# Stacked 128-row products in a delta-rule recurrence: two products over 64 rows each become one over 128

## The chip, the cores and the metric

The kernel runs on one core of one Trainium2 chip. The metric is the device time of a run in microseconds (us). The kernel before has a median of 845.26 us over three runs (835.6 to 846.0).

Engines are named as the profile names them: PE is the matrix engine (its weight loads have a row of their own, PEld), DVE the vector engine, ACT the scalar engine, POOL the general engine, SP the engine that issues most DMAs. PSUM is the memory that PE writes to; it is read by DVE and ACT.

## The reference, cut to what matters

Two blocks follow one another. The first is a recurrence over 768 time steps for 4 batches x 8 heads, with a 40 x 40 state per head:

```python
for t in range(S):
    y[:, :, t] = einsum('bhd,bhde->bhe', r_t, state)
    Sa = einsum('bhde,bhe->bhd', state, a_t)
    state = state * w_t[:, :, None, :] - einsum('bhd,bhe->bhde', Sa, b_t) + einsum('bhd,bhe->bhde', v_t, k_t)
```

The second takes the rows of y (3072 tokens of 320 numbers), routes each to the one of 8 experts whose gate logit is largest, and gives `gate_w * (relu(x @ w1[e]) @ w2[e])`. All of it is in fp32.

## The kernel before, in words

**Chunks and units.** The 768 steps are cut into 12 chunks (c) of 64 steps (T2). A unit is a chunk of two batches, so there are two units (s = 0, 1) in each chunk, 24 in all. A unit has 16 heads: 8 groups g times 2 parities par. Parity 0 lies on partitions 0 to 63 and parity 1 on partitions 64 to 127; `own(par)` is a parity's half and `oth(par)` the other half. Almost every matrix product is one head's: at most 64 rows (the contraction), 64 output partitions and 32 to 104 columns. `mm` (L228) records them all, so they share one line in the profile and are told apart by their output: ps_ntb, ps_gtk and so on. One product of fp32 shows as two MATMULs and two LDWEIGHTS. By the partitions of its input and of its output a product of 64 rows and 64 columns sits in one of four quadrants of the PE array.

**What a unit computes.** `decay` scans the decays (PT, on DVE), scales a by them into ai (POOL) and scales k and b by the reciprocals (DVE L287, POOL L290). Then:
- the system. `ntb` multiplies b with ai and an identity (16 products, 104 columns); its triangular part goes to pair (DVE L361), its other parts to off and nb (ACT L372, L374). `level` 0 to 4 (16 products each) squares and accumulates to invert the triangular system: PE into ps_lv, ACT copies to pair (L391), DVE transposes into N (L341) and adds (L394). `couple` and `whole` finish the inverse F. Systems need nothing of the state.
- the rest. `gtk` multiplies k with ai, giving GT and nk; `atv` multiplies v with r, giving AT and nv. `right` forms the right side q from the state and from GT, nv; `solve` and `zgram` give uT, u and ZT; `state` adds the products nk*nv and nb*u to the state (two products per head into one accumulation); `yield_y` adds three products per head (s*r, nk*AT, nb*ZT); its end copies y on ACT (L541) and scales it by PT on POOL (L542). `turned` transposes the state. `emit` turns y into token rows with the gate logits beside them, 16 products per unit, and sends them to x_rows with SP.

**The order of the work.** PE, DVE and ACT follow an order that is written out by hand. `weave` takes the system pieces of chunk c + 1 (16 pieces of 16 products: eight stages, two units each) and puts the products of chunk c's rest between them: after each two system products two of the rest, and what is left of the share of 26 after the piece. Tasks of `decay` for chunk c + 2 are put one after each piece from the third on. Eleven such woven steps follow one another; the last chunk's rest has no systems beside it. PE runs strictly in this order.

**PSUM.** Systems use the tag "two": two buffers of two banks, so that the two units take turns. The rest uses the tag "one": four buffers of one bank.

**After the recurrence** (L703 on) routing is computed, and from about 545 us on the experts run: layer1 (L859, L868), layer2 (L884).

Of the kernel before, what the change touches and what calls it, by code (L numbers as in the profile page):

```python
# [8 lines left out]
F32 = mybir.dt.float32  # L9
# [12 lines left out]
def kernel(  # L22
# [102 lines left out]
    with tc.tile_pool(name="ring", bufs=1) as ring, \  # L125
# [4 lines left out]

        G = 2 * NP
# [15 lines left out]
        kb_r = tiles("kb", 2, [128, 2, 2, NP, T2])  # L147
# [5 lines left out]
        nk_r = tiles("nk", 2, [128, G, 64])  # L153
# [38 lines left out]
        def preset_rest():  # L192
# [5 lines left out]
            for t in [r[0] for r in nk_r + q_r + st_r + s_r] + [r[1] for r in nk_r]:  # L198
                nc.gpsimd.memset(t[:, :, D:], 0.0)
# [5 lines left out]
        iw = ring.tile([128, NP, D + E], F32, name="iw")  # L205

        def preset_last():
            for par in range(2):
                nc.gpsimd.tensor_copy(iw[own(par), :, :D], i40[own(par), None, :].to_broadcast([64, NP, D]))
                nc.sync.dma_start(  # L210
                    iw[own(par, D), :, D:], moe_w_gate.rearrange("(p a e) x -> a e p x", p=NP, a=2)[par],
                )

        def wide(name):

            t = pp.tile([128, 2, 512], F32, name=name, tag="two", bufs=2)
            return t[:].rearrange("q b (g x) -> q (b g) x", x=128)

        def bank(name, w, gs=G):
            return pp.tile([128, gs, w], F32, name=name, tag="one", bufs=4)  # L220

        def halves(name):

            ps = [bank(name, T2 + D, NP) for _ in range(2)]
            return ps, lambda h, g: ps[g // NP][h, g % NP, :]
# [13 lines left out]
        def load(u):  # L239
# [7 lines left out]
            for b2 in range(2):  # L247
                src = packed[2 * s + b2, c * T2 // C, :, :, :, :, c * T2 % C : c * T2 % C + T2]
                for par in range(2):
                    for i, n in enumerate((K, B_)):  # L250
                        q.dma_start(d["kb"][own(par, D), b2, i], src[par, :, n])
                    q.dma_start(d["a"][own(par, D), b2], src[par, :, A])

        def load_vr(u):
# [4 lines left out]
            for b2 in range(2):  # L259
                src = packed[2 * s + b2, c * T2 // C, :, :, :, :, c * T2 % C : c * T2 % C + T2]  # L260
                for par in range(2):
                    gs = slice(b2 * NP, b2 * NP + NP)
                    nc.sync.dma_start(d["v"][own(par, D), gs], src[par, :, V])
                    nc.sync.dma_start(d["ri"][own(par, D), gs, :T2], src[par, :, R])

        def decay(u):
# [7 lines left out]
            def scan():  # L274
                PT = d["PT"] = sb.tile([128, G, T2 + 1], F32, name=f"PT{s}", bufs=3)
                d["wi"] = sb.tile([128, 2, NP, T2], F32, name="wi", bufs=2)
# [8 lines left out]
            def inverse(h, p):  # L285
                wi = d["wi"]
                nc.vector.reciprocal(wi[:, h, p : p + 2], by_batch(d["PT"][:, :, 1:])[:, h, p : p + 2])  # L287
                if p:
                    for i in (1, 0):
                        nc.gpsimd.tensor_tensor(d["kb"][:, h, i], d["kb"][:, h, i], wi[:, h], op=ALU.mult)  # L290
            return [scan] + [lambda h=h, p=p: inverse(h, p) for h in range(2) for p in range(0, NP, 2)]

        def kb(d, i, g):
            return d["kb"][:, g // NP, i, g % NP, :]


        def gtk(u):
# [3 lines left out]
            ps, at = halves("ps_gtk")  # L301
            ts = [lambda g=g, par=par: mm(at(oth(par), g), kb(d, 0, g)[own(par, D)], d["ai"][own(par, D), g, :])
                  for g, par in HD]

            def end():
                nk = d["nk"] = nk_r[s][c % 2]
                t = d["GT"] = sb.tile([128, G, T2], F32, name=f"GT{s}")
                for h in range(2):
                    gs = slice(h * NP, h * NP + NP)
                    nc.scalar.copy(t[:, gs], ps[h][:, :, :T2])  # L310
                    nc.scalar.copy(nk[:, gs, :D], ps[h][:, :, T2:])
                nc.gpsimd.tensor_tensor(t[:], t[:], up64[:, None, :].to_broadcast([128, G, T2]), op=ALU.mult)
            return ts, end

        def atv(u):
# [3 lines left out]
            ps, at = halves("ps_atv")  # L319
            ts = [lambda g=g, par=par: mm(at(oth(par), g), d["v"][own(par, D), g, :], d["ri"][own(par, D), g, :])  # L320
                  for g, par in HD]

            def end():
                nv = d["nv"] = sb.tile([128, G, D], F32, name=f"nv{s}")
                t = d["AT"] = sb.tile([128, G, T2], F32, name=f"AT{s}")
                for h in range(2):
                    gs = slice(h * NP, h * NP + NP)
                    nc.scalar.copy(nv[:, gs], ps[h][:, :, T2:])
                    nc.scalar.copy(t[:, gs], ps[h][:, :, :T2])
                nc.gpsimd.tensor_tensor(t[:], t[:], up64[:, None, :].to_broadcast([128, G, T2]), op=ALU.mult)  # L330
# [19 lines left out]
        def ntb(u):  # L350

            c, s = u
            d = units[u]
            ps = wide("ps_ntb")
            ts = [lambda g=g, par=par: mm(ps[oth(par), g, : T2 + D], kb(d, 1, g)[own(par, D)], d["ai"][own(par, D), g, :])
                  for g, par in HD]

            def end():
                old = new_pair(d, s)
                nt = d["nt0"] = old[:, :2]  # L360
                nc.vector.tensor_tensor(  # L361
                    parts(nt), ps[:, :, :T2].rearrange("q g (a t) -> q g a t", a=2),
                    nup[:].rearrange("q (a t) -> q a t", a=2)[:, None].to_broadcast([128, G, 2, 32]), op=ALU.mult,
                )
                new_n(d, s, nt)
                new = new_pair(d, s)
                nc.gpsimd.tensor_tensor(new[:, 2], old[:, 0], old[:, 1], op=ALU.add)
                nc.gpsimd.tensor_tensor(new[:, 2], new[:, 2], i32[:, None, :].to_broadcast([128, G, 32]), op=ALU.add)
                off = d["off"] = off_r[s][0]
                for par in range(2):  # L370
                    qs = own(par, 32)
                    nc.scalar.activation(off[qs, :, 32:], ps[qs, :, 32:T2], AF.Copy, scale=-1.0)  # L372
                t = d["nb"] = sb.tile([128, G, D], F32, name=f"nb{s}", bufs=2)
                nc.scalar.copy(t[:], ps[:, :, T2 : T2 + D])  # L374
            return ts, end

        def level(u, k):
# [7 lines left out]
                ps[oth(par), g, at].rearrange("q (a t) -> q a t", t=32), N[oth(par), g].rearrange("q a t -> q (a t)"), rhs[oth(par), :, g, :])  # L385
# [19 lines left out]
        def couple(u):  # L405
# [4 lines left out]
            ts = [lambda g=g, par=par: mm(ps[oth(par), g, :32], d["off"][oth(par), g, :], d["D"][oth(par), 0, g, :])  # L410
# [9 lines left out]
        def whole(u):  # L420
# [4 lines left out]
                ps[oth(par), g, :T2].rearrange("q (a t) -> q a t", a=2), d["x"][oth(par), g, :], d["TT"][oth(par), :, g, :])  # L425
# [10 lines left out]
        def right(us):  # L436

            pss = [bank("ps_q", D) for u in us]
            for u, ps in zip(us, pss):
                c, s = u  # L440
                d = units[u]
                if c:
                    yield [lambda g=g, par=par: mm(
                        ps[oth(par), g, :], d["ai"][own(par, D), g, :T2], st_r[s][0][own(par, D), g, :D],
                        start=(g == 0), stop=False, free=True) for g, par in HD], lambda ps=ps: parted(ps)
            for u, ps in zip(us, pss):
# [3 lines left out]
                def end():  # L450
# [3 lines left out]
                    ps[oth(par), g, :], d["GT"][oth(par), g, :], d["nv"][oth(par), g, :],  # L454
                    start=(c == 0), free=True) for g, par in HD], end

        def solve(u):

            c, s = u
            d = units[u]  # L460
            ps = bank("ps_uT", T2)
            ts = [lambda g=g, par=par: mm(ps[own(par), g, :], d["q"][oth(par), g, :], d["F"][oth(par), g, :])
                  for g, par in HD]

            def end():
                t = d["uT"] = sb.tile([128, G, T2], F32, name="uT", bufs=2)
# [527 lines left out]
```

## Time and profile before

| | before |
|---|---|
| median of 3 runs | 845.26 us (835.6 to 846.0) |
| the profiled execution, its own time | 844.75 us |
| its span in the profile | 843.0 us |
| mean granted PE clock | 0.954 |
| PE busy | 709.9 us, 84% of the span, 16816 MATMULs |
| DVE, ACT, POOL busy | 332.9, 282.6, 364.4 us |
| first system products of the woven steps | 66.9, 104.8, 145.4, 191.7, 236.5, 277.5, 319.5, 359.3, 402.4, 443.4, 485.5 us |
| last product of the last system | 524.2 us |

The profile page gives, for one execution, each engine's busy time and its share of the span; the span in 40 slices (busy tenths, and the granted PE clock in tenths of full speed); the DMA queues; the chain of work that ended last; and groups of instructions with count, busy time and mean duration, followed by the idle time before them and what ended it. "issue" stands for time in which an engine waited for nothing that the profile shows. Matmuls overlap, so the busy time of a group is less than its count times its mean. The windows view gives, for a stretch of time, its length, then the busy time and number of instructions of PE, PEld, DVE, ACT and POOL, the granted PE clock, the DMA share and GB/s.

### The profile page before, as it was taken

To read this page: it belongs to the slowest core of one execution; us is meant where nothing else is said; L and a number is where in the kernel's file an instruction comes from. 1 tells how busy PE (TensorE), PEld (TensorE's weight loads), DVE (VectorE), ACT (ScalarE), POOL (GpSimd) and SP (SyncE) were. 2 spreads that over 40 slices of the span, in tenths; PEclk is the share of its full clock that TensorE was granted. 3 is DMA by queue.
4 is the path that set the end of the run, shared out by engine and by line. 5 is a ranking of instruction groups with operands and counts; after the bars stand their busy time and mean duration, and the time that the engine had idled before them with its cause. 6 is when DMAs were issued, how large, how long until landed. Compare 5 with 4: busy or idle time off the path is not lost.

```text
span 843.0 us, 37380 instructions
## 1 busy us (share of the span) xinstructions
PE 709.9 (84%) x16816; PEld 576.3 (68%) x16816; DVE 332.9 (39%) x582; ACT 282.6 (34%) x752; POOL 364.4 (43%) x442
## 2 busy tenths in 40 slices
PE   0478898889897979888889898609999999999995
PEld 0478788889787979787879788604654655655653
DVE  2384565643746465656555642252110110120110
ACT  0236453534463636353636364300111111111110
POOL 9676655553656564655554633243203202111001
PEclk9998999976999999999998999858999999999998
DMA  4213132322222323232320110293325235232000
GB/s 105 51 43 76 44 87 55 86 50 52 59 63 63 74 45 76 51 70 51 70 51 23 35 23 5 54 318 93 105 81 176 90 95 170 79 96 90 16 7 24
DMA packets 123381, 61.20 MB, mean 73 GB/s; under 512 B 103697, under 2 KB 119059, under 8 KB 123220
## 3 DMA queue, kind: packets, MB, share of 16 engines
q1 hardware_dynamic: 112868, 48.34, 22.3%
q0 software_dynamic: 3136, 9.46, 3.6%
q8 instruction: 133, 2.18, 1.1%
q10 hardware_dynamic: 7216, 1.00, 0.7%
q14 instruction: 28, 0.23, 0.1%
HBM read 50.09 MB, written 9.32 MB: 70 GB/s over the span
## 4 chain that ended last, share of the span: by engine, by line
PE 48%; issue 35%; POOL 7%; DVE 4%; DMA 4%; ACT 1%; SPq 1%; POOLq 0%; ACTq 0%; DVEq 0%
PE ps_lv L228 11%; PE ps_y L228 6%; PE ps_ntb L228 5%; PE ps_q L228 4%; PE ps_atv L228 4%; PE ps_gtk L228 3%; POOL out_dram L889 3%; PE ps_f L228 3%; PE ps_z L228 3%; PE ps_x L228 3%; PE ps_S L228 2%; PE ps_uT L228 2%; PE ps_s L228 2%; POOL xg L836 1%; DMA w<-in_moe_w_dram 1%
## 5 line engine op out<-in xcount | busy, mean ns | idle before, releaser
L228 PE MATMUL ps_lv<-pair,N 64*64 64x96 f32 (+2 forms) x3840 | 201.6, 244 | 28.5 <-issue 19.4
L228 PEld LDWEIGHTS ps_lv<-pair,N 64*64 64x64 f32 x3840 | 171.1, 137 | 34.0 <-issue 24.5
L884 PE MATMUL zp<-w,h_sb 128*128 128x320 f32 (+1 forms) x512 | 124.1, 433 | 0.0
L889 POOL DMA_INDIRECT out_dram<-zo,s_idx x28 | 27.9, 998 | 210.3 <-ACT zo L888 209.7
L341 DVE STREAM_TRANSPOSE N<-pair 128x512 f32<-128x512 f32 x120 | 84.2, 701 | 66.2 <-ACT pair L391 64.9
L884 PEld LDWEIGHTS zp<-w,h_sb 128*128 128x128 f32 (+1 forms) x512 | 80.5, 177 | 37.1 <-issue 2.4
L874 DVE TENSOR_SCALAR h_sb<-hp 128x448 f32<-128x448 f32 x32 | 20.0, 625 | 209.3 <-PE hp L868 132.3
L868 PE MATMUL hp<-xgT,w 128*128 128x448 f32 x256 | 101.4, 549 | 0.0
L290 POOL TENSOR_TENSOR kb<-kb,wi 128x256 f32<-128x256 f32 x96 | 68.9, 739 | 56.2 <-DVE wi L287 52.2
L287 DVE RECIPROCAL wi<-PT 128x128 f32<-128x128 f32 x96 | 88.0, 921 | 0.1
L228 PE MATMUL ps_ntb<-ai,kb 40*64 40x104 f32 x768 | 62.4, 288 | 28.9 <-POOL ai L281 26.9
L868 PEld LDWEIGHTS hp<-xgT,w 128*128 128x128 f32 x256 | 47.8, 192 | 53.1 <-issue 53.1
L391 ACT COPY pair<-ps_lv 128x512 f32<-128x512 f32 x96 | 56.7, 590 | 77.4 <-PE ps_lv L228 65.0
L228 PEld LDWEIGHTS ps_ntb<-ai,kb 40*64 40x64 f32 x768 | 47.0, 154 | 29.5 <-POOL ai L281 26.9
L875 ACT ACTIVATE h_sb<-hp 128x448 f32<-128x448 f32 x32 | 17.4, 544 | 142.8 <-PE hp L868 87.6
L556 DVE TENSOR_REDUCE lg<-ps_x 128x16 f32<-128x64 f32 x24 | 5.4, 225 | 115.6 <-PE ps_x L228 114.1
L281 POOL TENSOR_TENSOR ai<-a,PT 128x512 f32<-128x512 f32 x24 | 28.4, 1182 | 51.7 <-DVE PT L277 37.2
L228 PE MATMUL ps_f<-TT,xt 64*64 64x64 f32 x768 | 48.4, 241 | 1.7 <-issue 1.1
L228 PE MATMUL ps_gtk<-ai,kb 40*64 40x104 f32 x768 | 46.0, 264 | 1.4 <-issue 1.3
L228 PE MATMUL ps_atv<-ri,v 40*64 40x104 f32 x768 | 42.7, 257 | 4.9 <-issue 3.9
L888 ACT ACTIVATE zo<-zp,xg 128x320 f32<-128x320 f32 x24 | 12.7, 528 | 100.0 <-PE zp L884 100.0
L228 PEld LDWEIGHTS ps_f<-TT,xt 64*64 64x64 f32 x768 | 42.0, 144 | 2.8 <-issue 1.1
(180 smaller groups left out, 1541.1 us busy)
## 6 DMA issues: line engine op xcount, KB each, us to landing
w<-in_moe_w_dram SPq DMA_DIRECT2D x8, 1280.0 KB
w<-in_moe_w_dram SPq DMA_DIRECT2D x8, 1024.0 KB
kb<-in_packed_dram SPq DMA_DIRECT2D x176, 40.0 KB
x_rows<-xr SPq DMA_DIRECT2D x48, 96.0 KB
v<-in_packed_dram SPq DMA_DIRECT2D x96, 40.0 KB
wp<-in_packed_dram SPq DMA_DIRECT2D x96, 40.0 KB
ri<-in_packed_dram SPq DMA_DIRECT2D x96, 40.0 KB
a<-in_packed_dram SPq DMA_DIRECT2D x88, 40.0 KB
```

The source lines that it names most:

```text
L228: nc.tensor.matmul(out_, lhsT=lhs, rhs=rhs, start=start, stop=stop, skip_group_check=free)
L281: nc.gpsimd.tensor_tensor(by_batch(d["ai"][:, :, :T2]), d["a"][:], by_batch(PT[:, :, :T2]), op=ALU.mult,)
L287: nc.vector.reciprocal(wi[:, h, p : p + 2], by_batch(d["PT"][:, :, 1:])[:, h, p : p + 2])
L290: nc.gpsimd.tensor_tensor(d["kb"][:, h, i], d["kb"][:, h, i], wi[:, h], op=ALU.mult)
L341: nc.vector.transpose(N[:].rearrange("q g a t -> q a g t"), nt)
L391: nc.scalar.copy(parts(new[:, :2]), ps[:, :, :T2].rearrange("q g (a t) -> q g a t", a=2))
L868: nc.tensor.matmul(hps[a][:, :cols], lhsT=w[0][:, db, f0 : f0 + 128], rhs=xT[:, db, :cols], start=(q % 2 == 1 and db == 0), stop=(q % 2 == ...
L874: nc.vector.tensor_relu(h[:, 2 * q, :cols], hps[0][:, :cols])
L875: nc.scalar.activation(h[:, 2 * q + 1, :cols], hps[1][:, :cols], AF.Relu)
L884: nc.tensor.matmul(zp[i * n : i * n + n], lhsT=h[:, fb, c0 : c0 + n], rhs=w[2][:, fb, :], start=(fb == 0), stop=(fb == FB - 1),)
L888: nc.scalar.activation(zo[:], zp[:], AF.Copy, scale=weight)
L889: ins_ = nc.gpsimd.indirect_dma_start(out=out[:, :], out_offset=bass.IndirectOffsetOnAxis(ap=idx, axis=0), in_=zo[:], in_offset=None, boun ...
```

## The change

The terms of k and of b are put on opposite halves of the partitions, so that products over both are one product of 128 rows instead of two of 64.

- `load` puts k and b side by side in one kb tile, in opposite order for the two parities; `load_vr` puts v and r on the other half. One POOL product per batch half scales k and b together.
- `grams` replaces ntb and gtk. Its 32 products per unit write two wide PSUM tiles, one per parity, in which the two terms lie on opposite halves. Both tiles are of the tag "sys", which has two buffers of two banks (the tag "two" of before). DVE multiplies twice, over 64 partitions each; ACT copies off, nkb and GT once per parity.
- `state` is one product of 128 rows per head (nkb * vu); `y_rest` one where yield_y had two (nkb * az); `emit` takes both parities in one product of 128 rows, 8 per unit. nkb, vu and az are stacks per parity, filled half by atv or grams and half by zgram.
- y is scaled by PT on DVE, straight out of PSUM.
- The rest uses wide tiles of the tag "rest", two buffers of two banks.
- `weave` spreads the rest's products evenly (19 for each piece). Batches of 128-row products (state, y_rest, emit) are kept whole and run only between pieces. A chunk's emit runs one chunk later. System stages alternate between the two units, as before; grams has 32 products.
- Quadrants change for several products: atv reads and writes the other half, right and levels write their own half.
- wi and acc have one buffer instead of two, y four instead of two.

```diff
-        kb_r = tiles("kb", 2, [128, 2, 2, NP, T2])
+        kb_r = tiles("kb", 2, [128, G, 2, T2])
...
-        def wide(name):
-            t = pp.tile([128, 2, 512], F32, name=name, tag="two", bufs=2)
+        def wide(name, tag="sys"):
+            t = pp.tile([128, 2, 512], F32, name=name, tag=tag, bufs=2)
             return t[:].rearrange("q b (g x) -> q (b g) x", x=128)
...
-                    for i in (1, 0):
-                        nc.gpsimd.tensor_tensor(d["kb"][:, h, i], d["kb"][:, h, i], wi[:, h], op=ALU.mult)
+                    kb = d["kb"][:, h * NP : h * NP + NP]
+                    nc.gpsimd.tensor_tensor(kb, kb, wi[:, h, :, None, :].to_broadcast([128, NP, 2, T2]), op=ALU.mult)
...
+        def grams(u):
+            c, s = u
+            d = units[u]
+            pss = [wide("ps_gram") for par in range(2)]
+            ts = [lambda g=g, par=par, i=i: mm(
+                pss[par][i * 64 : i * 64 + 64, g, : T2 + D], d["kb"][own(par, D), g, i, :], d["ai"][own(par, D), g, :])
+                for g in range(G) for i in range(2) for par in range(2)]
+            def end():
+                old = new_pair(d, s)
+                nt = d["nt0"] = old[:, :2]
...
+                for par, ps in enumerate(pss):
+                    nc.vector.tensor_tensor(
+                        parts(nt)[own(par)], ps[own(par), :, :T2].rearrange("q g (a t) -> q g a t", a=2),
+                        nup[own(par)].rearrange("q (a t) -> q a t", a=2)[:, None].to_broadcast([64, G, 2, 32]), op=ALU.mult,
+                    )
+                new_n(d, s, nt)
...
+                for par, ps in enumerate(pss):
+                    qs = own(par, 32)
+                    nc.scalar.activation(off[qs, :, 32:], ps[qs, :, 32:T2], AF.Copy, scale=-1.0)
+                    nc.scalar.copy(d["nkb"][par][:, :, :D], ps[:, :, T2 : T2 + D])
+                    nc.scalar.copy(t[oth(par)], ps[oth(par), :, :T2])
...
         def atv(u):
-            ps, at = halves("ps_atv")
-            ts = [lambda g=g, par=par: mm(at(oth(par), g), d["v"][own(par, D), g, :], d["ri"][own(par, D), g, :])
+            ps = wide("ps_atv", "rest")
+            ts = [lambda g=g, par=par: mm(ps[oth(par), g, : T2 + D], d["v"][oth(par, D), g, :], d["ri"][oth(par, D), g, :])
                   for g, par in HD]
...
         def state(us):
-                yield [lambda g=g, par=par: mm(
-                    ps[own(par), g, :], d["nk"][oth(par), g, :], d["nv"][oth(par), g, :],
-                    start=(g == 0), stop=False, free=True) for g, par in HD], none
...
-                yield [lambda g=g, par=par: mm(
-                    ps[own(par, D), g, :], d["nb"][oth(par), g, :], d["u"][oth(par), g, :],
-                    start=False, free=True) for g, par in HD], end
+                yield [lambda g=g, par=par: mm(ps[own(par), g, :], d["nkb"][par][:, g, :], d["vu"][par][:, g, :])
+                       for g, par in HD], end
...
+        def y_rest(us):
+                def end():
+                    t = d["y"] = sb.tile([128, G, T2], F32, name="y", bufs=4)
+                    nc.vector.tensor_tensor(t[:], ps[:], d["PT"][:, :, :T2], op=ALU.mult)
+                yield [lambda g=g, par=par: mm(
+                    ps[own(par), g, :], d["nkb"][par][:, g, :], d["az"][par][:, g, :],
+                    start=(c == 0), free=True) for g, par in HD], end
...
-        def rest(us, nx):
+        def rest(us, nx, before):
             last = us[0][0] + 1 == NS
-            ps = [right(us)] + [lambda u=u: gtk(u) for u in nx[:1]]
-            ps += [lambda u=u: solve(u) for u in us] + [lambda u=u: gtk(u) for u in nx[1:]]
-            ps += [lambda u=u: zgram(u) for u in us]
+            ps = [right(us), solve(us)] + [lambda u=u: zgram(u) for u in us]
+            if before:
+                ps += [(emit(before),)]
+            ps += [lambda u=u: atv(u) for u in nx]
             if not last:
-                ps += [state(us)]
-            ps += [yield_y(us)] + [lambda u=u: atv(u) for u in nx]
+                ps += [(state(us),)]
+            ps += [y_state(us), (y_rest(us),)]
             if not last:
-                ps += [lambda u=u: turned(u) for u in us]
-            return ps + [emit(us)]
+                ps += [turned(us)]
+            return ps
...
-                weave(systems(nx) if nx else [], rest(us, nx), 416, ahead, 2)
+                weave(systems(nx) if nx else [], rest(us, nx, pairs[c - 1] if c else []), 304, ahead, 2)
...
+            weave([], [(emit(pairs[-1]),)], 16, [])
```

## The prediction

> **What bounds the kernel now.** I read the page first (engines, then slices), then PE's waits, then the chain over some microseconds, then single steps of the recurrence as windows.
>
> ```profile
> PE 709.9 (84%) x16816; PEld 576.3 (68%) x16816; DVE 332.9 (39%) x582; ACT 282.6 (34%) x752; POOL 364.4 (43%) x442
> PEclk9998999976999999999998999858999999999998
> q8 instruction: 133, 2.18, 1.1%
> ```
> PE carries the span; no other engine passes 43%. The third line matters: 2.18 MB in 133 packets is 16.4 KB each, and 2 x 16816 PE instructions over 133 packets are 253 per packet. The next view shows what that does:
>
> ```profile
> PE ps_lv L228 <- issue: 19.4, 23, 1.5
> PE ps_y L228 <- issue: 13.3, 15, 1.5
> PE ps_s L228 <- issue: 8.6, 10, 1.4
> PE ps_lv L228 <- DVE pair L394: 4.4, 8, 1.3
> PE ps_lv L228 <- DVE N L341: 3.1, 2, 1.6
> ...
> ```
> ```profile
> 368.16 0.98 issue
> ...
> 372.43 1.12 issue
> ...
> 376.83 0.82 issue
> ...
> 380.44 1.26 issue
> ```
> In the recurrence PE waits for "issue" about every 4 us, some 1 us each time, and hardly ever for another engine. I read that as its own instruction stream: one 16 KB block per 253 instructions. A step has 1344 matmuls (2 per fp32 product) and as many weight loads, 2688 / 253 = 10.6 blocks in its 39.8 us: 3.75 us for each. All issue rows of PE's waits sum to 57 us, about 5 us per step.
>
> ```profile
> 319.50:359.30 39.80, 34.95 (x1352) 33.57 (x1346) 23.61 (x39) 20.54 (x60) 23.30 (x25) 1.00 0.28 64
> 191.70:236.50 44.80, 40.54 (x1351) 39.57 (x1350) 23.64 (x39) 20.56 (x59) 23.29 (x25) 0.85 0.25 57
> 181.00:204.90 23.90, 23.90 (x473) 23.90 (x468) 3.43 (x7) 8.59 (x24) 6.66 (x8) 0.50 0.21 48
> 177.60:181.00 3.40, 2.10 (x70) 1.90 (x66) 0.55 (x1) 2.13 (x7) 3.40 (x5) 1.00 0.01 1
> 443.90:447.20 3.30, 2.77 (x79) 2.63 (x77) 0.86 (x3) 0.58 (x2) 0.29 (x1) 1.00 0.27 62
> ```
> Windows, columns as in the page's engines. Row 1 is a clean step: 39.8 us, 1352 MATMUL records. Row 2 is a step that a stretch at half clock (row 3) hits. Rows 4 and 5 are the 3.4 us just before a drop of the clock: 70 and 79 matmuls, where 3.4 us of a clean step hold 115. So thin PE work halves the clock. Row 3: 473 matmuls should take 473 x 29.4 ns = 13.9 us and took 23.9: 0.42 us lost per us.
>
> ```profile
> 322.06 0.69 DVE L361 TENSOR_TENSOR pair<-ps_ntb,nup 128x512 f32<-128x512 f32 x1 [1.68 <-PE ps_ntb L228]
> 322.79 0.76 ACT L372 ACTIVATE off<-ps_ntb 32x256 f32<-32x256 f32 x2 [0.45 <-DVE pair L361]
> 323.56 0.43 ACT L374 COPY nb<-ps_ntb 128x320 f32<-128x320 f32 x1
> ```
> The emptying of one ps_ntb buffer: DVE first, ACT only after it, 1.9 us in all. It is hidden, since ps_ntb takes one of two buffers and the other unit's product fills the other.
>
> **What the skill says.** (1) "TensorE: Matmul & The Clock Gate", Part 1: an activity monitor with a window of 3.4 us gates the clock to half. Rows 2 to 5 agree. (2) "PSUM — Partial Sum Buffer", PSUM bank collisions: two engines must not touch one bank and quadrant at once, so accesses are ordered. Agrees: off waits for DVE pair in 23.4 of its 23.7 us. (3) "TensorEngine Tiling (Array Packing)", Key Properties: changing the tiling mode drains TensorE. In the expert layers matmuls of 128 rows start 376 ns apart; at a change to or from 64 rows the first two intervals are 469 and 473 ns, so about 0.19 us per change. (4) Same page: tiles run independently. Agrees: ps_z beside ps_lv (four different quadrants) run 4 matmuls in 91 ns; ps_q beside ps_ntb (the same two) 8 in 295 ns.
>
> **The change part by part**, for one step (two units); 11 steps are woven with the next step's systems.
>
> *Fewer products.* Before, 336 products per unit: ntb, gtk, couple, whole, solve, zgram, atv, turned, emit 16 each, levels 80, right 32, state 32, yield 48. After, 296: state 16, yield 32, emit 8. That is 80 products less per step, 160 of 1344 MATMULs (12%), 320 instructions. If the instruction stream set the pace everywhere: 320 / 253 x 3.75 = 4.7 us per step saved.
> PE's own work, without issue waits, is 39.8 - 5.0 = 34.8 us for 1344, 25.9 ns each; for 1184 it is 30.7.
>
> *Other quadrants.* atv now goes from oth to oth, the quadrants of the levels beside it, where it went across. 16 products per quadrant x 2 passes x 87 ns (a 104-column pass by the gaps in (4)) = 2.8 us that no longer overlap, about half of it inside time PE would spend issuing anyway: +1.4. The right product beside grams stays in a shared quadrant as it was: 0.
>
> *128-row batches.* No row of before has 64-column tiles with 128 rows; bounded by (3). emit, state and y_rest make six batches per step, each in and out: 12 x 0.19 = +2.3; at least 0 (drain hidden), at most 12 x 0.3.
>
> *grams takes both system buffers.* This is the main cost. grams allocates two wide tiles per unit of a two-buffer tag, so the second unit's grams waits until the first unit's are empty, with 3 products in between. After the last gram (0.31 us to its result): two DVE multiplies of 0.69 (rows count per partition, so 64 partitions cost as 128), the second under ACT; ACT starts at 1.04 and issues off, nkb, GT for one parity, then again. Its spacing in the ACT records is 0.39 for off, 0.32 for 320 elements, 0.48 for 512; end at 1.04 + 2 x (0.39 + 0.32 + 0.48) + 0.1 = 3.5 us. PE idles 3.3 us. The first level then needs the second grams' first buffer: 0.31 + 0.73 + 0.39 + 0.32 + 0.59 = 2.35, idle 2.1 us. The second buffer is ready while that level runs. And the second gram of a step waits for F of the last whole (0.25 + 0.59): +0.7. Queued behind each is everything on PE, in order; nothing else can fill. Sum +6.1; low end 3, if copies start earlier than I set them, high end 8.
>
> *ACT queue.* z and atv are emptied in four copies (2 x 320, 2 x 512: 1.6 us) where 1.1 us stood; a level's pair copy (L391, 590 ns) queues behind, then the transpose (L341, 701 ns), then the next level. +1.0, from 0 to 2.5. DVE gains y (0.69 per unit) and a second gram multiply, 2.8 us on 23.6 of 39.8: hidden. POOL loses the y product (1182 ns) and merges two kb products of 739 into one of about 1270: off the path. SP: v, ri and kb only change their partitions; x_rows issues the same four DMAs a step, earlier than load_vr instead of just before it: 0. wi with one buffer can hold DVE's reciprocals for POOL, 0 as POOL has 16 us to spare per step.
>
> *Sum without clock effects:* 30.7 + 1.4 + 2.3 + 6.1 + 1.0 = 41.5 us. The instruction stream catches up in the idle stretches; I leave 0 for it. Before: from the first ntb of the woven steps (66.9) to 524.2 are 457.3 us; less the two half-clock losses (10.0 and, for 148 matmuls in 6.7 us, 2.3) 445 over 11 is 40.5. So +1.0 per step, +11 us.
>
> *Clock.* 3.3 us idle, 2.5 us of grams, 2.1 us idle: a 3.4 us stretch there holds fewer than the 70 to 79 matmuls that preceded a drop. I take a drop in 9 of 10 steps, lasting 7 to 10 us (6.7 was the shortest): grams of the second unit takes 2.4 us longer, the first level 1.0, so 3.4 x 0.9 = +3.1 per step, +34. The two losses of before (12.3) stand in its time: +22 net.
>
> *Ends.* Start: first gram 0.5 later (one kb product of 1270 against 739), two gram emptyings 1.5 longer each: +3.5. End: y by DVE saves ACT 0.59 + POOL 1.18 - 0.69 = 1.1; the deferred last emit about cancels it. Expert layers (545 to 843 us) untouched.
>
> Total: 844.75 (span 843.0) + 11 + 22 + 3.5 = 881. The median shown, 845.26, is 0.5 above the profiled execution; I keep 881.
>
> **Rivals.**
> A (forecast, chance 0.5): as above, 881, from 862 to 905.
> B, no clock loss (0.22): the grams idle, but the clock stays or falls no oftener than before: 845 + 11 + 3.5 = 860 less some of the high bounds, 840 to 862; it ends within 2% mostly. For: other thin windows kept their clock. Against: none held so little.
> C, faster (0.15): the instruction stream still sets the pace because the gram emptying is short or lies inside its waits. It decides from where the new idle stays under about 3 us a step: saved 4.7, paid mode changes 2.3 and nothing else: -2.4 x 11 = -26, 819 (with hidden drains 793). For: issue waits are the only regular ones now. Against: a wait of 3.3 us is longer than any issue wait (1.5).
> D, clock stays low (0.13): drops last as in row 3, 24 us of each step: 0.42 x 24 = 10 us less what waits hide, +6 x 11: 925.
>
> **Numbers.** Likeliest 881. Range 828 to 915: leaves out most of C (0.12) and the upper half of D (0.08). 2% (17 us) is about what a measurement of this kernel can tell: faster 0.14, same 0.24, slower 0.62.
>
> **What would show it.** MATMUL and LDWEIGHTS at about 14960 each (928 products less over all units); PE waits on ACT at ps_gram near 3 us, 11 times, and at ps_lv near 2; issue waits falling from 57 to under 25 us; PEclk below 9 once per step; step length near 44 us. Wrong if PE's gram waits are under 1 us, or if the clock holds 1.0 through them, or if changes to 128 rows cost nothing.

## The result, and the profile after

The changed kernel took 969.59 us (median of 4 runs, 969.38 to 971.79), the kernel before beside it 845.63 us. The ratio is 1.152, 95% interval 1.142 to 1.162. The forecast was slower, 881 us, with a range up to 915: the side was right, the time lies outside the range, and the loss is about three and a half times the one forecast (+124 instead of +36).

The page of the changed kernel first, its lines for the engines, the granted PE clock and PE's instruction stream:

```profile
PE 761.2 (79%) x14960; PEld 604.7 (62%) x14960; DVE 372.0 (38%) x642; ACT 318.5 (33%) x704; POOL 346.6 (36%) x395
PEclk9995979797988888796979696965599999999998
q8 instruction: 118, 1.93, 0.9%
```

There are 1856 MATMULs less, and yet PE is busy 51 us longer: the second line says why, since the clock falls once in each woven step. The instruction blocks fell with the instructions, from 133 to 118.

PE's waits in the changed kernel (total us, how often, longest us):

```profile
PE ps_gram L229 <- ACT GT L323: 30.2, 22, 2.1
PE ps_lv L229 <- ACT GT L323: 26.7, 13, 3.4
PE ps_lv L229 <- DVE pair L380: 14.8, 20, 1.6
PE ps_x L229 <- DVE lg L534: 12.4, 12, 1.5
PE ps_s L229 <- DVE acc L482: 9.4, 10, 0.9
PE ps_uT L229 <- ACT uT L451: 8.8, 12, 0.9
PE ps_S L229 <- ACT s L495: 7.8, 11, 0.8
PE ps_gram L229 <- ACT F L416: 7.5, 11, 1.7
PE ps_q L229 <- ACT q L438: 6.1, 12, 0.5
PE ps_y L229 <- ACT seen L236: 5.6, 19, 0.5
PE ps_q L229 <- ACT seen L236: 3.5, 12, 0.3
```

All waits for "issue" together are 4.5 us now, where they were 57. In their place stand waits for ACT and DVE, of two kinds. Rows 1, 2 and 8 are the ones that the prediction named (the emptying of the grams, and F). The rows at ps_x, ps_s, ps_uT, ps_S, ps_q and ps_y are waits of the *rest*, 53.6 us in all, 4.9 per step, and the prediction named none of them. Each is a wait of the second unit's product for the emptying of the first unit's result: ps_uT waits for the copy out of ps_uT, ps_s for the addition out of ps_s (`seen` is ACT's copy of one element out of the tile). The diff suggests the cause: the changed kernel's `banks` puts the results of both units into one tile of two banks (tag "rest"). If the order is kept per tile and not per bank, the second unit has to wait; the first experiment tests this.

One step of the changed kernel as windows (length; PE, PEld, DVE, ACT, POOL busy; clock, DMA share, GB/s): the whole step and its stretch at half clock:

```profile
377.70:428.20 50.50, 39.34 (x1192) 35.75 (x1189) 26.99 (x44) 23.77 (x54) 21.97 (x20) 0.83 0.22 50
381.00:398.30 17.30, 11.88 (x273) 10.85 (x272) 5.91 (x8) 6.99 (x18) 5.45 (x6) 0.51 0.17 39
```

The second row holds only 273 matmuls in 17.3 us and PE is busy 11.9 us of it: a stretch with much waiting, which is also slow while it works. The emptying of the grams inside it, in order of time on ACT (start, duration, what):

```profile
382.84 0.37 ACT L321 ACTIVATE off<-ps_gram 32x256 f32<-32x256 f32 x1 [1.70 <-DVE pair L311]
383.12 0.40 ACT L322 COPY nkb<-ps_gram 128x320 f32<-128x320 f32 x1
383.53 0.58 ACT L323 COPY GT<-ps_gram 64x512 f32<-64x512 f32 x1
384.01 0.37 ACT L321 ACTIVATE off<-ps_gram 32x256 f32<-32x256 f32 x1
384.40 0.43 ACT L322 COPY nkb<-ps_gram 128x320 f32<-128x320 f32 x1
384.72 0.58 ACT L323 COPY GT<-ps_gram 64x512 f32<-64x512 f32 x1
```

That is the sequence of six operations that the prediction set up. PE's gaps in the matmul records there are 1.98 us (to the end of the first GT), 0.58 (to the end of the second), and 1.90 before the first level.

Where the clock falls is read from the 3.4 us before a fall, as the prediction did. The first row is the step shown, the second the step after it:

```profile
377.80:381.20 3.40, 2.66 (x100) 2.26 (x91) 0.00 (x0) 1.07 (x3) 0.00 (x0) 1.00 0.08 19
432.40:435.80 3.40, 0.60 (x12) 0.40 (x16) 2.05 (x3) 2.44 (x6) 1.63 (x3) 1.00 0.30 67
```

Of the nine falls inside the ten steps, seven come as in the second row, after a wait for the grams of about 2 us; one, at 128.6, comes inside such a wait. In the step shown the clock falls at 381.2, a us before that wait begins (382.18), after 100 matmuls and no gap longer than 0.59 us. So the waits for the grams stand before most falls, and not before all, and the 70 to 79 matmuls of the prediction are no limit.

Where the 125 us of span went is read from three times in each trace: the first system product of the first woven step, that of the last woven step, and the end of the last product of emit (ps_x). Beside before and after stand three kernels of the experiments below.

| us | before | after | own banks | own banks, filler | own banks, grams by groups |
|---|---|---|---|---|---|
| up to the first woven step | 66.9 | 72.6 | 75.8 | 77.1 | 67.6 |
| ten woven steps | 418.6 | 509.7 | 470.6 | 444.2 | 449.6 |
| one of them, mean | 41.9 | 51.0 | 47.1 | 44.4 | 45.0 |
| of the ten, at half clock | 32 | 162 | 146 | 32 | 104 |
| last woven step and last chunk | 56.5 | 85.5 | 62.9 | 61.7 | 57.8 |
| routing and experts, to the end | 301.0 | 299.9 | 303.4 | 303.6 | 300.6 |

So 91 us come from the ten steps, 29 from the last step and the last chunk (whose rest has no systems beside it to cover a wait; 47.7 of its 85.5 us ran at half clock, none of before's), 6 from the start, and the experts are untouched.

### The profile page after: what moved, and what is told of

Same layout as the page of the kernel before. It is cut to its first block, busy times and chain, and to the rows that moved or that the text cites. A ratio compares the mean times of both kernels' runs of the same rounds, so it can differ in the third digit from the quotient of the medians.

```text
span 967.7 us, 33578 instructions
## 1 busy us (share of the span) xinstructions
PE 761.2 (79%) x14960; PEld 604.7 (62%) x14960; DVE 372.0 (38%) x642; ACT 318.5 (33%) x704; POOL 346.6 (36%) x395
## 5 line engine op out<-in xcount | busy, mean ns | idle before, releaser
L229 PE MATMUL ps_lv<-pair,N 64*64 64x96 f32 (+2 forms) x3840 | 222.9, 263 | 44.4 <-ACT GT L323 26.7
L229 PEld LDWEIGHTS ps_lv<-pair,N 64*64 64x64 f32 x3840 | 195.1, 153 | 51.3 <-ACT GT L323 29.1
L229 PE MATMUL ps_gram<-ai,kb 40*64 40x104 f32 x1536 | 107.5, 342 | 63.8 <-ACT GT L323 30.2
L229 PEld LDWEIGHTS ps_gram<-ai,kb 40*64 40x64 f32 x1536 | 85.9, 178 | 70.4 <-ACT GT L323 34.3
L291 POOL TENSOR_TENSOR kb<-kb,wi 128x512 f32<-128x512 f32 x48 | 61.1, 1273 | 114.4 <-DVE wi L288 109.5
L311 DVE TENSOR_TENSOR pair<-ps_gram,nup 64x512 f32<-64x512 f32 x48 | 33.0, 689 | 171.7 <-PE ps_gram L229 170.9
L469 POOL TENSOR_TENSOR az<-az,up 128x512 f32<-128x512 f32 x48 | 59.6, 1274 | 32.3 <-ACT az L468 32.1
L229 PE MATMUL ps_q<-vu,GT 64*64 64x40 f32 x768 | 62.6, 301 | 9.4 <-ACT q L438 6.1
L229 PE MATMUL ps_atv<-ri,v 40*64 40x104 f32 x768 | 67.0, 255 | 0.7 <-DMA ri<-in_packed_dram 0.7
L229 PEld LDWEIGHTS ps_q<-vu,GT 64*64 64x64 f32 x768 | 57.5, 218 | 13.2 <-ACT q L438 8.3
L229 PE MATMUL ps_q<-st,ai 40*64 40x40 f32 x704 | 58.7, 246 | 2.3 <-issue 0.7
```

Source lines behind the costliest of these rows:

```text
L229: nc.tensor.matmul(out_, lhsT=lhs, rhs=rhs, start=start, stop=stop, skip_group_check=free)
L291: nc.gpsimd.tensor_tensor(kb, kb, wi[:, h, :, None, :].to_broadcast([128, NP, 2, T2]), op=ALU.mult)
L311: nc.vector.tensor_tensor(parts(nt)[own(par)], ps[own(par), :, :T2].rearrange("q g (a t) -> q g a t", a=2), nup[own(par)].rearrange("q (a ...
```

## The experiments

The experiments were measured in several groups, with the kernel before beside each group; its medians were 834.5 to 845.7. Differences between kernels of different groups are read only where they are larger than these 11 us, or from the traces.

### Own banks for each unit in the rest

```diff
+        def bank(name, w, gs=G):
+            return pp.tile([128, gs, w], F32, name=name, tag="one", bufs=4)
...
-            t = pp.tile([128, 2, 512], F32, name=name, tag="rest", bufs=2)
-            return [t[:, i, : G * w].rearrange("q (g x) -> q g x", x=w) for i in range(2)]
+            return [bank(name, w)[:] for _ in range(2)]
...
-            ps = wide("ps_atv", "rest")
+            ps, at = halves("ps_atv")
```

(`zgram` likewise; both are then emptied in two halves, as in the kernel before.)

> The changed kernel, but each unit's product of the rest has PSUM banks of its own again (four buffers of one bank, atv and zgram in two halves of four groups); quadrants, batches and order stay. Theory 1, that two units in one two-bank tile make the second unit's product wait until the first unit's is emptied: in the changed kernel PE waits for lg, acc, uT, s, q and seen add to 54 us, 4.9 per step; they go to under 10 us, time 915 to 930. Rival, that the wait of grams for its own buffers and the half clock behind it are all: those waits only move elsewhere, 960 to 970.

Measured: 912.75 us (910.95 to 914.54), ratio to before 1.083 (1.076 to 1.091): 57 us less than the changed kernel, a little more than the theory said. PE's waits:

```profile
PE ps_gram L234 <- ACT GT L328: 28.6, 22, 2.1
PE ps_lv L234 <- ACT GT L328: 26.8, 13, 3.4
PE ps_lv L234 <- DVE pair L387: 19.0, 19, 1.9
PE ps_y L234 <- DVE D L390: 15.6, 20, 1.2
```

The waits of the rest are gone, those for the grams stay as they were, and the levels and `couple` now wait more for DVE. The table shows the gain: 39 us in the ten steps and 23 after them, less 3 at the start and 3.5 in the experts (55 of span). That settles the largest part of the loss: it is the shared tile, with the half clock that went with it (16 us less of it in the ten steps, 34 less after them).

### The grams cut by parity, and both edits together

```diff
-        def grams(u):
+        def grams(u, par):
...
-            pss = [wide("ps_gram") for par in range(2)]
+            ps = wide("ps_gram")
...
-            return ([lambda: grams(u)] + [lambda k=k: level(u, k) for k in range(5)]
+            return ([lambda: grams(u, 0), lambda: grams(u, 1)] + [lambda k=k: level(u, k) for k in range(5)]
```

> The changed kernel, but grams is cut into two pieces of 16 products, one per parity and buffer, with the other unit's piece between, so that a buffer is emptied while the next piece runs. Theory 2, that grams holding both buffers makes PE idle (57 us on ACT GT) and that this idle sends the clock to half: PE waits for GT fall to under 20 us, fewer half clock stretches, time 890 to 915. Rival, that the shared tiles of the rest set the pace: less than 20 us gained, 950 to 969.

Measured: 1026.61 us (1024.62 to 1028.59), slower by 57 instead of faster. The waits for GT did go (from 30.2 and 26.7 to 1.0 at ps_lv, none at ps_gram), but the ten steps spent 253 us at half clock instead of 162, and the rest waited longer for its shared tile (ps_q for seen 22.2 us instead of 3.5). The pieces of 16 products of one parity use only one row half of the array; that this is what kept the clock down was not tested by itself.

> The first two edits together. Theories 1 and 2 add up: 969 - 50 - 70 = about 850, steps of 40 us. If the two wait for the same thing one after the other, the gain is that of the larger alone, 890 to 920.

Measured: 902.28 us (896.5 to 908.06), only 10 below own banks alone. The two edits don't add: half clock is still 138 us of the ten steps.

### Work that is only there to keep PE busy

44 products per step whose results nobody reads (they go to free columns of ps_q), put where PE waits for the grams, in every woven step but the first:

```diff
+                if fill and n < 2:
+                    filler(n)
```

> The changed kernel with 44 added products per step, whose results nobody reads, put where PE waits for grams and for the first level (28 and 16 of 128 columns, about 3.1 and 1.8 us). The waits stay, but PE's array works through them. Theory 3, that the clock falls because of these waits and costs 0.42 us per us of half clock (14 to 17 us per step): full clock in nearly all steps, 900 to 915. Rival, that half clock hides behind the waits for ACT and DVE: 965 to 985, the added products cost a little.

Measured: 938.91 us (937.25 to 940.56): 31 less than the changed kernel, about half of what I had expected. The clock was held (half clock 46 us of the ten steps instead of 162), so the expectation failed on the price of half clock: the ten steps are 27.0 us shorter for 116 us less of it, 0.23 per us. The fillers' own time is in that, so 0.23 is a lower bound.

> Own banks per unit, and the added products in the two waits of grams (44 per step, unread). Full clock in nearly all steps. On the changed kernel they gained 31 us; the same here: 878 to 890. If the clock only mattered together with the other waits: 905 to 915.

Measured, on own banks: 885.94 us (883.58 to 888.3), 27 below own banks alone, as expected. The clock line of its page:

```profile
PEclk9985789999999999999999999975999999999998
```

And one of its steps as a window:

```profile
390.50:434.60 44.10, 38.08 (x1284) 35.72 (x1278) 26.15 (x44) 25.72 (x71) 21.99 (x20) 1.00 0.25 56
```

Full clock through whole steps, with more matmuls than the kernel without fillers (1284 instead of some 1200), and 2.6 us less per step in the mean of the ten. This kernel shows what the change costs without the shared tile and with no more half clock than before: 44.4 us per step, the fillers' own time included, against 41.9.

### The grams cut by groups

Each half takes four of the eight groups and both parities, so it uses all four quadrants and needs one buffer instead of two:

```diff
-            pss = [wide("ps_gram") for par in range(2)]
+            ps = pp.tile([128, 2, 512], F32, name="ps_gram", tag="sys", bufs=2)
...
-                for g in range(G) for i in range(2) for par in range(2)]
+                for g in range(NP) for i in range(2) for par in range(2)]
```

> The changed kernel, but grams is cut by groups into two pieces of 16 products (four groups each, both parities, all four quadrants); each fills one buffer, the other unit's piece lies between, and DVE and ACT empty each piece in twice as many operations of half the size. The cut by parity before it had kept each piece in two quadrants and got slower at half clock; if that was the reason, theory 2 holds here: PE's long waits for GT (57 us) shrink below 20 us, time 905 to 930. If the waits of grams are not worth their length, 955 to 975.

Measured, on the changed kernel: 987.26 us (984.85 to 989.68), slower than it by 18 and outside both expectations. Its waits:

```profile
PE ps_q L229 <- ACT seen L236: 29.6, 21, 2.7
...
PE ps_uT L229 <- ACT uT L459: 18.0, 12, 1.9
```

The grams wait no longer, but now the shared tile of the rest is waited for in the same place, and longer (seen at ps_q 3.5 before the edit, uT at ps_uT 8.8), since ACT has the copies of the grams queued in front of it; half clock is 212 us of the ten steps. The pieces lie in all four quadrants here, so one row half of the array was not the whole reason of the half clock in the cut by parity.

> Own banks per unit in the rest, and grams cut by groups. Theories 1 and 2 add: 912 - 40 = 870 (855 to 885), steps of 42 us, about those of the kernel before. If the two don't add: 895 to 912.

Measured, with own banks: 879.96 us (877.59 to 882.33), ratio 1.054 (1.034 to 1.075), 33 below own banks alone. The same edit gains or loses, then, by whether the next wait behind it is there. By the table 8 of the 33 come at the start, 21 in the ten steps, 5 at the end. Two of its steps show that what is left is uneven:

```profile
338.90:380.70 41.80, 35.39 (x1190) 33.47 (x1184) 26.61 (x48) 26.98 (x82) 22.27 (x20) 0.96 0.26 60
380.70:428.90 48.20, 41.41 (x1205) 39.30 (x1198) 26.61 (x48) 27.24 (x83) 22.27 (x20) 0.82 0.23 53
```

The first, nearly at full clock, takes as long as a mean step of the kernel before; the second, with the same work, 6.4 us more at a clock of 0.82. That is 13.7 us more at half clock, so 0.47 us per us, twice what the fillers gave. Taken over the nine later steps: 41.9 us with 3.5 at half clock, 43.9 to 44.5 with 7 to 10, 47.3 to 48.1 with 17 to 20, so about 0.4 per us. The ten steps have 72 us more of half clock than before; at 0.4 that would be 29 of the 31 us by which they are longer, which is an estimate and was not tested. PE no longer waits at ps_gram for GT here; 8 of the 15 falls in the ten steps come after a wait of about 1.3 us at ps_y for D. No kernel here with the change in it is clearly faster than this one, and it is still slower than the kernel before.

### The price of a change between 64 and 128 rows

Own banks, with the 128-row products put one by one between the 64-row products of the systems, 779 changes in the recurrence instead of 131:

```diff
-                ps += [(emit(before),)]
+                ps += [emit(before)]
...
-            ps += [y_state(us), (y_rest(us),)]
+            ps += [y_state(us), y_rest(us)]
```

> Own banks per unit, and the 128-row products no longer kept in batches but laid between the system products as the other rest products are: changes between 64 and 128 rows rise from 131 to 779. At 0.13 us each, the gap that the trace of the run with own banks shows at a change, 648 x 0.13 = 84 us, less what waits hide: 960 to 1000. At the 0.19 us of the forecast: 1010 to 1040. If a change costs nothing: 900 to 920.

Measured: 1025.07 us in the profiled run and 1045.32 in the other. By the profiled run that is 112 more for 648 changes, 0.17 us each; but its half clock was longer too (228 us of the ten steps instead of 146). So the same again on the kernel with fillers:

> The kernel with own banks and the unread filler products, which keeps full clock, and the 128-row products scattered among the 64-row ones: 648 more changes of the array between 64 and 128 rows, this time with the clock held up. Theory (a change costs 0.13-0.15 us, as gaps in the traces show it): 885.94 rises by 84 to 97, to 970-983. Rival (0.19 as the expert layers' intervals show): 1000-1015. Rival (much of the 122 us of the run without filler was its longer half clock): below 950.

Measured: 988.4 us (982.99 to 990.6), 102.5 more: 0.16 us each, outside all three expectations. But the clock was not held: the ten steps have 109 us of half clock instead of 32, so this figure holds both. The price of a change alone is read from steps at full clock. One of three:

```profile
404.00:454.30 50.30, 47.02 (x1288) 40.71 (x1280) 27.97 (x44) 26.01 (x71) 20.79 (x20) 1.00 0.22 51
```

Each step has 72 changes instead of 12. The three steps (50.3, 49.8 and 49.7 us) are 6.4 us longer than the seven of the filler kernel at full clock (43.5 in the mean), 0.11 us for each of 60 changes; PE is busy 9 us longer in them (47.3 for 38.3 in the mean), 0.15 each, and the difference falls into time in which PE waited before. So a change takes about 0.15 us of PE's time, as the first theory had it; the rest of the 102.5 us, about 30, goes with the longer half clock. Six batches per step are then 12 x 0.15 = 1.8 us.

### Fewer batches

On own banks and grams by groups, emit and state of both units in one stretch, y_rest of both in one, 47 changes instead of 131:

```diff
+        def joint(n, *gens):
...
-            if before:
-                ps += [(emit(before),)]
+            ps += [(joint(16 * bool(before) + 32 * (not last), *([emit(before)] if before else []), *([] if last else [state(us)])),)]
```

> The kernel with own banks and the grams cut by groups, and the 128-row batches of a step joined: emit of both units and state of both units in one stretch, y_rest of both units in one, so 47 changes between 64 and 128 rows in the program instead of 131. Theory: 84 changes x 0.15 us (the 122 us of the run with scattered 128-row products, less some 24 us for its longer half clock, over 648 changes) = 12.6 us less than 879.96, 862-871. Rival (a batch of six hides in waits of the levels, and long stretches hold the levels back): 876-892.

Measured: 903.26 us (901.0 to 904.97), 23 slower than with six batches, beyond even the rival. The view of PE's waits says where:

```profile
PE ps_lv L234 <- DVE pair L395: 43.2, 26, 3.5
```

This wait was 12.2 us with six batches. Nine of the 26 last 3.5 us each, 31.8 in all, and come in the same place of each step. What DVE does in one of them (PE waits from 136.37 to 139.90):

```profile
137.61 1.23 DVE L283 TENSOR_TENSOR_SCAN PT<-wp,first 128x520 f32<-128x520 f32 x1
138.76 0.69 DVE L369 STREAM_TRANSPOSE N<-pair 128x512 f32<-128x512 f32 x1
139.37 0.39 DVE L395 TENSOR_TENSOR pair<-ps_lv,pair 128x256 f32<-128x256 f32 x1
```

The transpose and the sum that PE waits for stand behind this scan, and the scan behind the four state operations of both units (135.57 to 137.69), which the joined stretch put into DVE's queue together. So the joining shows how the order of DVE's work sets this wait. That a batch between two pieces also covers the emptying of the piece before it is likely, but not shown by it.

### Other quadrants, and y

`atv` back to products that cross from one half to the other, for which v and a second copy of r lie on the other rows (only one such copy is kept, so the first chunk's products take the second chunk's r, and wait 8.5 and 11.2 us for it in the two kernels; that is left out of the reading. The y of the first chunk is therefore wrong in these two kernels, while the work is the same in kind and amount):

```diff
-                    nc.sync.dma_start(d["v"][oth(par, D), gs], src[par, :, V])
+                    nc.sync.dma_start(d["v"][own(par, D), gs], src[par, :, V])
+                    nc.sync.dma_start(d["ra"][own(par, D), gs, :T2], src[par, :, R])
...
-            ts = [lambda g=g, par=par: mm(at(oth(par), g), d["v"][oth(par, D), g, :], d["ri"][oth(par, D), g, :])
+            ts = [lambda g=g, par=par: mm(at(oth(par), g), d["v"][own(par, D), g, :], d["ra"][own(par, D), g, :])
```

> The kernel with own banks for the rest, and atv back on crossing quadrants (v and a second copy of r on the rows opposite to its output, so that it lies beside the levels in four different quadrants). My prediction priced the lost crossing at 1.4 us per step. Theory: 912.75 falls by about 15, to 893-902. Rival (these passes lie in time that PE would spend issuing anyway): 906-916.

Measured, on own banks: 920.78 us (916.33 to 922.3), 8 more, which the trace has at the start; the woven steps are 47.3 us against 47.1. No gain.

> The kernel with own banks, grams cut by groups, joined 128-row batches, and atv on crossing quadrants. Theory: both gains add, 15 us less than the kernel with joined batches alone, 847-857. Rival (crossing quadrants buy nothing where PE is held by waits and by half clock): no different from the kernel with joined batches, within 5 us.

Measured, on the joined batches: 898.51 us (896.83 to 899.32), 5 less, with the start's wait in it; the woven steps fell from 47.1 to 45.9. Between nothing and 1.1 us per step: which of the two a given order shows stays open.

y back to a copy on ACT and a multiply on POOL, on own banks and grams by groups:

```diff
-                    nc.vector.tensor_tensor(t[:], ps[:], d["PT"][:, :, :T2], op=ALU.mult)
+                    nc.scalar.copy(t[:], ps[:])
+                    nc.gpsimd.tensor_tensor(t[:], t[:], d["PT"][:, :, :T2], op=ALU.mult)
```

> The kernel with own banks and the grams cut by groups, and y back to a copy on ACT and a multiply on POOL (the one part of the change that moves work between engines, undone). My prediction costed it at nothing: DVE has room. Theory: no difference from 879.96 that a measurement can tell, 872-888. Rival (y on DVE stands ahead of the levels' sums and transposes, and the waits of the levels on DVE shrink with it gone): 855-870. Other rival (ACT's copy stands ahead of the pair copies, which is why the change moved it): 890-900.

Measured: 880.26 us (870.83 to 882.32) against 879.96. The ten steps are 450.8 us against 449.6. Where y is scaled makes no difference that these runs can tell, and the levels' wait for pair hardly changes (9.2 us for 12.2).

## Why the prediction was right in its direction and wrong in its size

**The tile of the rest: the step that failed.** The sum had no term for it. That the rest uses wide tiles of two banks stood in the description of the change, and the prediction put its cost at nothing without a reason. Its nearest term, the ACT queue (+1.0 us per step), looked at how many copies ACT has and not at which tile they free. In the changed kernel PE waits 4.9 us per step for the shared tile; own banks undid this and gained 3.9 us per step and 23 us in the last step and chunk, where nothing covers it: 57 us in all. Of the 88 us between 881 and 969.6 that is the largest part.

**ACT queue: right beside the shared tile, too small without it.** In the changed kernel PE waits 14.8 + 1.6 us for pair and D, where before it waited 4.4 + 1.3: about 1 us per step more, as forecast. With own banks the same two waits are 19.0 + 15.6, 3.1 us per step over eleven. That the products saved were also the cover of these waits (19 products of the rest per piece instead of 26) fits this, but is argued: no run changed that number alone.

**Other quadrants, Fewer products, 128-row batches: the work on PE.** Together they were forecast to leave 34.4 us of work per step (30.7 + 1.4 + 2.3), 0.4 less than before. The step of 41.80 us shown above has PE busy 35.39 us with 3.4 us at half clock, so between 33.7 and 35.4 at full clock; the clean step of before had 34.95. Within it the changes of rows measured 1.8 for 2.3, and the quadrants 0 to 1.1 for 1.4. So this part was right as far as the traces can tell: 160 MATMULs less per step gain PE almost nothing here, since the other two parts give most of it back. The issue waits fell to 4.5 us where "under 25" was asked for. Rival C asked for less than 3 us of new idle time per step, and the grams alone brought 5.1.

**Grams takes both system buffers: right in size.** Forecast were 3.3, 2.1 and 0.7 us of idle time, 6.1 in all. In the step shown they are 2.56 (1.98 and 0.58, since the second unit's products for the first tile start when that tile is empty), 1.90 and 0.59: 5.1.

**Clock: near in its sum, by some luck.** A drop was forecast in 9 of 10 woven steps, and there is one in each. In the nine after the first step it lasts 13.7 to 17.1 us and not 7 to 10. In the nine steps that have fillers, holding the clock gained 3.1 us per step on the changed kernel and 2.9 on own banks, against the 3.1 forecast. The fillers' own time is in that, so it is a lower bound, and their price of 0.23 us per us stands beside about 0.4 between steps of one kernel: that a longer drop was offset by a lower price is the reading of the fillers alone. The reason given, idle time at the grams, fits eight of the nine falls. It doesn't fit the step shown, nor the 104 us of half clock that stay with own banks and the grams cut by groups, where half of the falls come after shorter waits for D; how little work makes the clock fall stays open.

**Ends: wrong.** +3.5 was forecast for the start, and 5.7 came before the first woven step; with own banks it is 8.9, and with the grams cut by groups 0.7, so this excess belongs to the grams. The 11th woven step and the last chunk came to +29, where the step's own +4 and about nothing else had been set; with own banks they are +6.4, so most of this is the shared tile again.

The remaining 31 us, from 881 to own banks' 912.75, are in the main the woven steps (47.1 for 44.6, of which the first alone is 51.8) and the start (8.9 for 3.5).

## What to carry to other kernels

Products saved on PE are worth little when new waits take their place: here PE's own work per step stayed where it was, and the waits decided. Before merging products, list for each result which tile holds it, who reads the tile, and who writes it next, and give each such wait a term in the sum. In this kernel a tile that holds two producers' results is one resource: the second producer waits for the first one's reader even though they lie in different banks. And a repair can be judged only with the next wait removed too: cutting the grams lost 18 us beside the shared tile and gained 33 without it.

## What the runs showed of the hardware that I had not expected

- The clock fell without PE ever being idle for long. The Trainium skill, "TensorE: Matmul & The Clock Gate", Part 1, gives half clock as the state after an idle window of about 3.4 us. In the changed kernel no gap of PE in the 3.4 us before the nine falls inside the ten steps was longer than 2.06 us, and in the step shown the longest was 0.59. The clock then stayed at half for 13.7 to 17.1 us; 44 more products per step were enough to hold it at 1.00 through most steps.
- What half clock costs depends on the kernel: 0.23 us per us by the fillers, twice (27.0 us for 116, and 26.3 for 114, the fillers' own time included), and about 0.4 between steps with the same work in the kernel with own banks and grams by groups. The prediction had 0.42 from the kernel before.
- A change between 64 and 128 rows takes about 0.15 us of PE's time in the recurrence, of which 0.11 shows in the length of a step; the prediction read 0.19 from the expert layers. "TensorEngine Tiling (Array Packing)", Key Properties, says that a change of mode drains the engine, without a price.
- The "issue" waits, which the prediction read as waits for the instruction stream, nearly vanish when PE waits for others: with 11% fewer PE instructions they fell by 92%, from 57 to 4.5 us. The stream was caught up on in the new idle time, as I read it; in the kernel with own banks and fillers, where PE waits less, they are 16.9 us.
